# Windowed attention with two feed-forward stages on one Trainium2 core: diagonal matrices off GpSimd, weight remainders onto it, a third place for early scores, another idle fill

## Chip, core and metric

The kernel runs on one core of one Trainium2 chip. TensorE (PE in the profile), VectorE (DVE), ScalarE (ACT), GpSimd (POOL) and SyncE (SP, which issues most transfers) each work through a queue of their own in order. The metric is device time in microseconds (us) from a run of the whole program; lower is better.

## What is computed

Three layers follow one another, all in float32 from inputs that arrive partly as 64-bit floats:

```python
# attention: batch 4, 8 heads, 576 positions, 64 per head, window 64
scores = q @ k.T / sqrt(64)            # masked: 0 <= row - col < 64
attn = softmax(scores)                 # denominator + 1e-9
x = (attn @ v), heads side by side     # (4, 576, 512)
# first feed-forward stage
x_prev = x shifted by one position
xk = mu_k * x + (1 - mu_k) * x_prev
xr = mu_r * x + (1 - mu_r) * x_prev
k = relu(xk @ w_k)                     # 512 -> 1024
x = sigmoid(xr @ w_r) * (k * k @ w_v)  # 1024 -> 512
# second stage
gate = sigmoid(causal 5-tap convolution of x, per channel)
out = (gate * (x @ w_val)) @ w_out
```

## The kernel before

All 2,304 positions are cut into five blocks: t = 0 with 256 positions, then four of 512. In each block the attention has four units (one for two heads), so unit u = 0 to 3 belongs to block 0, u = 4 to 7 to block 1, and so on. A unit is a chain of small steps: `qk` (TensorE: scores with the mask added), `top` (VectorE: row maximum), `exp` (ScalarE), `eps` (one addition to the sums), `rec` (VectorE: reciprocal). In block 0 `diag` then makes diagonal matrices of the reciprocals, `tp` (TensorE) multiplies the scores by them, which transposes and normalizes at once, `pt` copies the result out of PSUM, `pv` (TensorE) multiplies by v and `x` copies the result to `xT`. In later blocks `norm` and a VectorE transpose `tr` take the place of `diag`, `tp` and `pt`.

The first stage of block t then needs, for each of xk and xr and each half g of the channels, `a` (the scaling by mu) and `xm` (VectorE: the mix with the shifted row). From block 1 on the mixed rows are split in a rounded part (`xhi`) and its remainder (`xlo`), and TensorE runs three float32r products; block 0 runs plain float32 products straight from the converted weights. The products are named r (w_r), h (w_k) and v (w_v); product m of block 0 comes in two halves.

Weights come as ten pieces: `ld` loads 64-bit words, `t` (VectorE shift), `g` (ScalarE) and `s` (VectorE) make float32 of them, `hi` rounds them and `lo` subtracts the rounded part from the whole, which gives the remainder. Only blocks 1 to 4 need `hi` and `lo`.

The order of everything is written out by hand: the table `SLOT` gives each step a place in one long list, and a letter says which engine takes it where there is a choice (a ScalarE, v VectorE, p GpSimd). The class `Plan` walks through that list, issues each step on its engine, and at the same time keeps its own estimate of the time; from that it decides where TensorE would wait for more than 400 ns, and calls `fill` there, which issues products of zeros into an unused PSUM tile. The estimates set nothing but the number of these. The scores of block 0 and of units 4 and 5 go into PSUM tiles of a pool `p0` with two buffers, but for unit 5, which has `s4`. When all of these are read, the pool is closed and its place becomes the four banks `pg` of the products.

Of the kernel before, what the change touches and what calls it, by code (L numbers as in the profile page):

```python
# [20 lines left out]
P = 128  # L21
# [22 lines left out]
    'first': '0',  # L44
    'warm': '1',
    'cap': '3',
    'ident': '2',
    'band': '13',
    'low': '4',
    'table': '12',  # L50
    'ldmu': '7',
    'ldc': '92',
    'mu': '51',
    'omu': '52',
    'pg': '79',
    'wc0': '323 250 326',
    'wc': '327',
    'first_x': '6',
    'ldqk': '8 9 10 14 16 49 101 127 161 150 195 256 328 338 367 414 406 433 461 528',
    'ldv': '15 30 60 68 87 110 139 181 289 235 305 322 386 390 432 453 507 505 550 607',  # L60
    'qk': '18 21 22 36 45 69 103 148 187 241 257 337 350 373 389 431 452 508 520 540',
    'top': '19 23 29 53 62 77 140 178 262 267 283 347 366 404 422 443 460 524 541 554',
    'exp': '20 25 33 55 71 78 147 191 269 281 297 355 375 408 428 454 468 531 552 557',
    'eps': 'v24 p26 v41 p59 p88 p112 p175 p192 v270 v282 v311 p365 v380 v410 p439 v464 p488 p543 p558 p565',
    'rec': '27 35 50 64 91 138 176 198 271 285 312 368 381 411 447 466 516 544 568 583',
    'diag': 'v28 p40 p57 p67',
    'tp': '34 44 61 73',
    'pt': 'v37 a46 v66 v82',
    'pv': '38 48 70 83 128 166 200 223 294 313 356 378 412 436 481 499 535 563 573 614',
    'x': 'v47 a56 v81 a84 a136 a182 a216 a238 v298 a317 a357 v384 v415 v444 a486 a502 a536 a567 a578 a643',  # L70
    'norm': 'v95 v154 v179 v215 v272 v306 a340 a371 a382 a426 v448 v495 v517 v545 v569 v595',
    'tr': '96 158 184 219 273 308 348 372 399 427 449 496 533 551 572 604',
    'mask': '107 160 194 246 274 344 354 374 405 434 459 513 534 553',
    'edge': '126 171 218 264 280 345 360 376 413 437',
    'a': 'a65 a85 a89 a113 a225 a228 a244 a248 a333 v334 a392 v393 a465 v471 a521 v523 a605 a610 a686 v711',
    'xm': '75 98 108 114 236 237 277 251 349 346 403 395 478 476 547 538 622 663 690 738',
    'xlo': '76 100 137 120 240 243 321 255 364 391 441 397 512 518 587 577 677 708 724 783',
    'carry': '118 123 278 295 363 420 522 570',
    'r': '80 105 86 121 93 119 102 116 336 339 342 352 462 483 501 494 655 695 681 692 801 824 826 827',
    'sig': '115 124 129 135 341 358 370 388 477 487 515 519 676 696 697 698 816 825 837 838',  # L80
    'h': '149 153 146 159 143 151 145 152 169 177 174 189 185 196 183 197 290 287 268 279 296 307 314 302 '
        '416 435 407 421 450 467 463 479 599 594 600 611 618 613 667 653 749 748 778 766 780 784 804 818',
    'relu': 'a155 a163 a157 a162 a204 a205 a206 a210 a291 a292 a286 a293 v318 v320 a331 a332 a442 a451 a429 '
        'v430 a474 a485 v484 a497 a602 v603 v617 a624 a649 v657 a668 v669 a756 v758 a779 a791 a793 v796 '
        'a817 a821',
    'sbuf': '164 165 208 211',
    'slo': 'a202 a203 a209 a212 310 325 330 353 472 480 503 510 629 642 684 679 792 808 829 828',
    'v': '220 230 213 233 226 253 254 259 359 383 361 377 401 417 400 402 525 555 537 561 566 580 514 532 '
        '712 735 699 710 706 720 747 752 866 884 831 851 843 853 860 882',
    'x2': '263 247 258 260 387 379 425 409 559 571 588 564 742 723 733 763 892 888 887 889',  # L90
    'st': '276 284 369 303 418 398 445 473 575 584 630 582 769 743 772 774 950 959 1000 987',
    'xhi': 'a239 a242 v319 v252 v362 v385 v440 a396 a511 a500 a576 a546 a672 v700 a716 v757',
    'cut': '232 249 343 394 475 530',
    'shi': '300 315 324 335 456 457 491 498 621 625 660 670 762 795 797 822',
    'sq': 'a301 a316 v329 a351 v469 a470 a492 v506 v628 a627 a683 a678 a777 v805 a819 v823',
    'staging': '5',
    'w_r ld': '11 42',
    'w_r g': '32 58',
    'w_r t': '31 63',
    'w_r s': '39 72',  # L100
    'w_r hi': 'a43 v90',
    'w_r lo': '54 94',
    'w_k ld': '104 74 125 131',
    'w_k g': '111 97 141 142',
    'w_k t': '117 106 156 170',
    'w_k s': '122 109 168 172',
    'w_k hi': 'v130 a134 a214 a222',
    'w_k lo': '180 144 227 229',
    'w_v ld': '133 132 173 193',
    'w_v g': '186 167 221 231',  # L110
    'w_v t': '188 190 199 217',
    'w_v s': '207 201 224 245',
    'w_v hi': 'a275 v288 a261 a265',
    'w_v lo': '309 304 299 266',
    'wide_x': '234',
    'turn': '836',
    'turn_s': '895',
    'turn_w': '865 845',
    'w_val ld': '542 562 597 647',
    'w_val room': '585 631 615 646',  # L120
    'w_val g': '586 633 619 654',
    'w_val t': '590 593 601 596 606 581 635 637 636 638 612 644 651 626 652 659 665 673 682 680',
    'w_val s': '592 634 620 661',
    'w_val hi': 'v608 a639 v662 a688',
    'w_val lo': '609 645 671 691',
    'w_val st': '616 632 648 658 666 675 717 705',
    'w_out ld': '640 694 740 746',
    'w_out room': '674 703 744 786',
    'w_out g': '687 704 745 787',
    'w_out t': '713 715 718 722 719 702 729 730 732 750 770 775 785 781 788 755 800 806 807 810',  # L130
    'w_out s': '714 721 771 798',
    'w_out hi': 'a726 v760 v789 a813',
    'w_out lo': '736 761 790 815',
    'w_out st': '759 751 767 773 809 802 814 835',
    'wv2': '867 839',
    'wo2': '902 880 881 848',
    'ldx': '841 904 926 1001',
    'gbuf': '871 922 1040 1034',
    'ldg': '873 949 1043',
    'xhi_': 'a846 v883 v855 a852 a879 a877 a910 a925 a909 a923 a948 a940 a972 a1056 a966 a982 a1002 a1009 a1075 '  # L140
        'a1106 a1077 a1090 v1124 v1105',
    'xlo_': '847 899 856 858 900 878 916 962 915 928 953 946 981 1061 991 983 1035 1021 1080 1118 1096 1102 '
        '1138 1110',
    'xsum': '842 849 859 876 906 911 924 934 958 964 994 1007 1070 1088 1103 1104',
    'val': '885 886 898 901 905 912 914 919 927 935 944 954 974 980 989 1066 999 1008 1028 1073 1044 1086 1098 '
        '1109 1114 1120 1135 1146',
    'valu': 'a891 a903 a907 a929 a945 a960 a996 a1016 a1031 a1100 a1112 a1127',
    'valc': '893 913 917 921 933 965 975 993 1068 1039 1082 1054 1108 1130 1140 1165',
    'gv': '894 920 918 932 973 978 986 1011 1069 1067 1089 1055 1164 1157 1142 1170',
    'ghi_': 'v896 a936 a930 a939 a943 a956 a967 a995 a1012 a1004 a992 a1006 a1022 a1025 a1093 a1062 a1101 v1113 '  # L150
        'a1116 v1144 a1132',
    'glo_': '897 937 979 942 947 971 968 1010 1026 1027 998 1015 1029 1033 1097 1072 1136 1122 1119 1145 1133',
    'gsum': '931 941 951 955 988 1003 1019 1024 1095 1115 1128 1131',
    'out': '908 952 963 969 976 985 997 1018 1030 1032 1048 1058 1081 1078 1099 1085 1123 1141 1143 1150 1156 '
        '1183 1185 1184 1188 1162 1168 1167 1173',
    'outu': 'a938 a970 a977 a1023 a1053 a1071 a1107 a1137 a1147',
    'o': '957 984 990 1005 1045 1074 1087 1079 1117 1148 1155 1163 1186 1189 1175 1169 1179',
    'os': '961 1017 1014 1037 1060 1076 1139 1092 1152 1158 1161 1171 1187 1190 1177 1174 1180',
    'oa': '1013 1051 1050 1064 1126 1125 1153 1178 1172',
    'tap': '1036 1041 1047 1038 1042 1052 1059 1065 1091 1046 1057 1084',  # L160
    'part': '1049 1020 1083 1111',
    'acc': '1063 1094 1121 1134',
    'gate': '1129 1154',
# [1167 lines left out]
```

## Time and profile before

| | |
|---|---|
| median of 3 runs (lowest, highest) | 413.92 us (413.46, 414.34) |
| the profiled execution: its time | 413.41 us |
| its span, first to last instruction | 411.5 us |
| TensorE busy | 402.6 us, 98% of the span |
| VectorE busy | 340.5 us, 83% |
| ScalarE busy | 261.5 us, 64% |
| GpSimd busy | 38.3 us, 9% |

Times in the rows below are microseconds from the start of the span unless marked ns. A matmul that the program issues in float32 stands twice in the trace, as two passes. [...]

### The profile page before, as it was taken

The page shows a single profiled execution, that of the slowest core. Times are in us where ns is not written, and L with a number is a line of the kernel's source. Part 1 is how long each engine was busy: PE and PEld are TensorE (multiplying, and loading weights), DVE is VectorE, ACT ScalarE, POOL GpSimd, SP SyncE. Part 2 cuts the span into 40 slices and gives each one's busy share as a digit, 9 for nine tenths or more (in the row PEclk, how much of TensorE's full clock was granted, in tenths as well). Part 3 has the DMA queues.
Part 4 walks back from the last instruction along what each step waited for, and adds up shares of the span by engine and source line. Part 5 has one row for each costly group of instructions (what it writes and reads, how often), then busy time and mean ns, then how long its engine had stood idle before and what let it go on. Part 6 is the DMA issues. An engine that isn't in the chain of part 4 may idle for free.

```text
span 411.5 us, 10921 instructions
## 1 busy us (share of the span) xinstructions
PE 402.6 (98%) x4587; PEld 342.1 (83%) x4587; DVE 340.5 (83%) x503; ACT 261.5 (64%) x607; POOL 38.3 (9%) x87
## 2 busy tenths in 40 slices
PE   8899999999999999999999999999999999999995
PEld 4678888887778778877888888888888999999995
DVE  4899999798548489789898899788885999999960
ACT  4889995778884767686556653156322476977531
POOL 3920101000100011000000000000000001123110
PEclk9999999999999999999999999999999999999999
DMA  7998911214323342262266428564999727869664
GB/s 284 411 414 339 328 46 57 78 44 145 107 74 129 98 125 77 78 223 92 80 242 263 149 89 291 208 235 156 405 395 382 261 86 245 228 142 198 137 149 128
DMA packets 24674, 78.37 MB, mean 190 GB/s; under 512 B 3376, under 2 KB 6704, under 8 KB 21808
## 3 DMA queue, kind: packets, MB, share of 16 engines
q1 hardware_dynamic: 22608, 72.64, 48.8%
q0 software_dynamic: 1872, 5.01, 7.3%
q8 instruction: 36, 0.59, 0.6%
q14 instruction: 14, 0.11, 0.1%
q10 hardware_dynamic: 144, 0.00, 0.0%
HBM read 51.80 MB, written 23.49 MB: 183 GB/s over the span
## 4 chain that ended last, share of the span: by engine, by line
PE 95%; POOL 3%; DVE 1%; ACT 0%; issue 0%; ACTq 0%; POOLq 0%
PE v L683 22%; PE h L683 21%; PE r L683 11%; PE sv L596 5%; PE h L706 4%; PE v L706 4%; PE sv L551 3%; PE val1m L961 3%; PE val3m L961 3%; PE out L1073 3%; PE out2m L961 3%; PE out1m L961 3%; PE val2m L961 3%; PE out0m L961 3%; PE val0m L961 3%; POOL rk L451 2%
## 5 line engine op out<-in xcount | busy, mean ns | idle before, releaser
L683 PE MATMUL h<-x,wk 128*128 128x512 f32 x384 | 90.5, 392 | 0.0
L683 PEld LDWEIGHTS h<-x,wk 128*128 128x128 f32 x384 | 71.6, 188 | 15.0
L683 PE MATMUL v<-sh,wv 128*128 128x512 f32 x256 | 82.4, 394 | 0.0
L683 PEld LDWEIGHTS v<-sh,wv 128*128 128x128 f32 x256 | 48.0, 188 | 10.8
L427 ACT ACTIVATE s<-s,m 128x96 f32<-128x96 f32 x120 | 43.0, 362 | 12.6 <-DVE m L416 11.5
L683 PE MATMUL v<-sl,wv 128*128 128x512 f32 x128 | 49.9, 390 | 0.0
L683 PE MATMUL r<-x,wr 128*128 128x512 f32 x192 | 45.8, 393 | 0.0
L683 PEld LDWEIGHTS r<-x,wr 128*128 128x128 f32 x192 | 35.7, 188 | 7.8
L892 DVE SCALAR_TENSOR_TENSOR early<-early,wc 128x576 f32<-128x576 f32 x48 | 38.5, 813 | 3.2 <-ACT early L890 2.7
L733 ACT ACTIVATE rk<-h 128x512 f32<-128x512 f32 (+1 forms) x30 | 15.4, 534 | 25.4 <-PE h L683 21.9
L683 PEld LDWEIGHTS v<-sl,wv 128*128 128x128 f32 x128 | 24.0, 188 | 4.7
L596 PEld LDWEIGHTS sv<-pt,vt 32*64 32x64 f32 x1536 | 18.9, 130 | 6.0 <-issue 3.9
L427 ACT ACTIVATION_READ_ACCUMULATOR s<-s,m 128x1 f32 x120 | 22.8, 190 | 0.0
L643 DVE SCALAR_TENSOR_TENSOR xm<-xT,omu,xm 128x512 f32<-128x512 f32 x32 | 22.3, 745 | 0.4 <-POOL xT L649 0.3
L666 DVE TENSOR_TENSOR x<-xm,x 128x1024 fp32r<-128x1024 f32 x16 | 19.5, 1219 | 3.6 <-ACT x L663 3.5
L785 DVE TENSOR_TENSOR sgs<-v,sgs 128x512 f32<-128x512 f32 (+1 forms) x20 | 12.5, 633 | 11.5 <-PE v L683 10.9
L763 DVE TENSOR_TENSOR sl<-rk,sh 128x1024 fp32r<-128x1024 f32 x16 | 19.5, 1221 | 2.4 <-ACT rk L761 2.2
L596 PE MATMUL sv<-pt,vt 32*64 32x32 f32 (+2 forms) x1536 | 20.8, 238 | 0.3 <-issue 0.3
L584 DVE STREAM_TRANSPOSE pt<-s 128x768 f32<-128x768 f32 x16 | 15.6, 973 | 5.1 <-ACT s L439 4.8
L757 ACT ACTIVATE sh<-rk 128x1024 fp32r<-128x1024 f32 x16 | 16.8, 1055 | 1.0 <-DVE rk L735 0.9
L896 ACT ACTIVATE early<-early 128x1152 f32<-128x1152 f32 x6 | 7.0, 1169 | 15.8 <-DVE early L892 15.8
L773 ACT ACTIVATE sgs<-r 128x512 f32<-128x512 f32 (+1 forms) x20 | 10.5, 552 | 8.2 <-PE r L683 8.1
(212 smaller groups left out, 828.0 us busy)
## 6 DMA issues: line engine op xcount, KB each, us to landing
qk<-qk SPq DMA_DIRECT2D x16, 544.0 KB, 5.1
vt<-vh SPq DMA_DIRECT2D x16, 384.0 KB, 3.9
xb<-x2d SPq DMA_DIRECT2D x4, 1152.0 KB, 6.7
out_t<-st SPq DMA_DIRECT2D x15, 288.0 KB, 2.9
w_out<-w SPq DMA_DIRECT2D x8, 512.0 KB, 3.4
w_val<-w SPq DMA_DIRECT2D x8, 448.0 KB, 3.1
wk<-w_val SPq DMA_DIRECT2D x2, 1792.0 KB, 8.8
early<-x2d SPq DMA_DIRECT2D x6, 576.0 KB, 4.4
```

What stands on the lines that cost most here:

```text
L427: ACT.activation(out=s, in_=scores()[:, 2 * c // n_s, c % (n_s // 2), :] if scores else s, func=AF.Exp, scale=D ** -0.5 if scores else 1.0 ...
L584: V.transpose(out=a["pt"][:, :m2 * KW], in_=a["s"].rearrange("p c j -> p (c j)"))
L596: PE.matmul(a["o"][heads[h], i, j0 * HW:j1 * HW], lhsT=a["v"][r, k, heads[h]], rhs=p, start=k == 0, stop=k == m + 1, skip_group_check=True)
L643: V.scalar_tensor_tensor(out=m, in0=xT[:, f, :n], scalar=omu[:, c:c + 1], in1=m, op0=ALU.mult, op1=ALU.add)
L666: lambda E: E.tensor_tensor(out=dst(1), in0=src(), in1=f32(dst(0)), op=ALU.subtract))
L683: PE.matmul(ps, lhsT=a, rhs=b[:, kt, :], start=(kt == 0 and i == 0), stop=(kt == nk - 1 and i == 2))
L706: PE.matmul(Ps[key][:, :n], lhsT=ws(kt), rhs=x()[:, kt, :], start=kt == 0, stop=kt == nk - 1)
L733: ACT.activation(out=o, in_=ps, func=AF.Relu)
L757: ACT.activation(out=Ss[t][0][:, f, :n], in_=rk(), func=AF.Square)
L763: lambda E: E.tensor_tensor(out=Ss[t][1][:, f, :n], in0=rk(), in1=f32(Ss[t][0][:, f, :n]), op=ALU.subtract))
L892: V.scalar_tensor_tensor(out=o, in0=x, scalar=c, in1=o, op0=ALU.mult, op1=ALU.add)
L961: PE.matmul(z[bank][:, j, :HS], lhsT=lhs, rhs=rhs, start=new and kt == 0 and e == 0, stop=kt == 1 and e == 2, skip_group_check=not new)
```

## The change

Six things change, and the diff shows them in this order.

- The table of places and letters is new throughout. `diag` of units 1 to 3 goes from GpSimd to VectorE, so all four are there. The remainder `lo` goes to GpSimd for both pieces of w_r, two of w_k and two of w_v; before, all ten were on VectorE.
- `masks` also copies a block of zeros into a part of `wr[1]` that is written for good only later.
- In `weight`, `lo` may run on VectorE or GpSimd. In `softmax`, `diag` may run on ScalarE or VectorE; no letter in the table picks ScalarE.
- The scores of units 2 and 5 use `s4`, those of 0, 1, 3 and 4 the two buffers of `p0` (function `space`). Products may take the place of `p0` once units 0 and 3 are read, and those with m > 1 of block 0 wait for units 1 and 4 instead.
- `tp` no longer waits for the `pv` before it; `pt` does.
- `fill` runs only in the stage before the later units, writes to the tiles of `tp` and `pv`, and past 6 us, when neither tile is held and no product is in PSUM, it multiplies halves of 64 rows by 256 columns of float32r zeros in place of 128 rows by 512 columns of bf16.

```diff
-    'diag': 'v28 p40 p57 p67',
-    'pt': 'v37 a46 v66 v82',
+    'diag': 'v27 v42 v49 v62',
+    'pt': 'v38 v50 a63 a79',
...
-    'w_r lo': '54 94',
+    'w_r lo': 'p69 p116',
...
-    'w_k lo': '180 144 227 229',
+    'w_k lo': 'v224 p203 p232 v226',
...
-    'w_v lo': '309 304 299 266',
+    'w_v lo': 'v347 v270 p294 p264',
...
+        G.tensor_copy(wr[1][:, NF - 1, :TA], warm)
     op("cap", "pool", 1300, ["warm"], masks)
...
-        vg((key, "lo"), n, [(key, "hi")],
-           lambda E: E.tensor_tensor(out=dst[1], in0=s(), in1=f32(dst[0]), op=ALU.subtract))
+        rest = lambda E: E.tensor_tensor(out=dst[1], in0=s(), in1=f32(dst[0]), op=ALU.subtract)
+        plan.any((key, "lo"), [(key, "hi")], ("dve", v_ns(n), lambda: rest(V)), ("pool", 8000, lambda: rest(G)))
...
-                 ("pool", 1300, lambda: [G.tensor_scalar(out=o, in0=ident, scalar1=l(1)[:, c:c + 1], scalar2=None, op0=ALU.mult)
-                                         for o in [diag()] for c, o in enumerate([o[:, c] for c in range(n_s)])]),
+                 ("act", 290 * n_s, by_act),
...
+    def space(u):
+        return Q["s4"] if u % 3 == 2 else p0.tile([P, 2, TB], F32, tag="p0", name=f"qk{u}")
...
-            a["ps"] = p0.tile([P, 2, TB], F32, tag="p0", name=f"qk{u}")
+            a["ps"] = space(u)
...
-        op(("tp", u), "pe", 870, [("diag", u), *([("pv", u - 1)] if u else [])], tp, ring=("pa", ("pt", u)))
+        op(("tp", u), "pe", 870, [("diag", u)], tp, ring=("pa", ("pt", u)))
...
-        plan.any(("pt", u), [("tp", u)],
+        plan.any(("pt", u), [("tp", u), *([("pv", u - 1)] if u else [])],
...
-    op("pg", "none", 0, [("exp", u) for u in range(HP + 1)], products)
+    op("pg", "none", 0, [("exp", 0), ("exp", 3), After(("exp", 1)), After(("exp", 4))], products)
...
-        if "pg" in Q:
-            if "spare" not in Q:
-                Q["spare"] = Q["pg"].tile([P, TB], F32, tag="g", name="spare")
-            ps = Q["spare"]
-        elif "ps" not in A[HP + 1]:
-            ps = Q["s4"][:, 0]
-        elif len(held) < 2:
-            ps = Q["pv" if "tp" in held else "tp"]
-        else:
+        if "sv" in Q or len(held) > 1:
             return
-        zero = warm.bitcast(BF16)
-        for _ in range(n):
-            PE.matmul(ps[:, :TB], lhsT=zero[:, :P], rhs=zero, start=True, stop=True)
+        ps = Q["pv" if "tp" in held else "tp"]
+        if len(Ps) or held or t < plan.COLD:
+            zero = warm.bitcast(BF16)
+            for _ in range(n):
+                PE.matmul(ps[:, :TB], lhsT=zero[:, :P], rhs=zero, start=True, stop=True)
+            return
+        zero = wr[1][:, NF - 1, :TA]
+        for i in range(n):
+            r = slice(i % 2 * W, i % 2 * W + W)
+            PE.matmul(Q["pv" if i % 2 else "tp"][:, :TA], lhsT=zero[r, :P], rhs=zero[r], start=True, stop=True)
```

Line numbers move by 8 to 15 in the changed file: VectorE's `diag` is L453 before and L464 after, its remainder L375 and L382.

How the order on three engines moves. On GpSimd, from the end of the masks, before (`first_m` and `m` hold the sums of a unit, `rk` the diagonal matrices, `s` the scores of a later unit):

```order
L324 COPY band<-cap 32x96 x4
L432 TENSOR_SCALAR first_m<-first_m 128x4
L451 TENSOR_SCALAR rk<-ident,first_m 128x128 x8
L432 TENSOR_SCALAR first_m<-first_m 128x4
L451 TENSOR_SCALAR rk<-ident,first_m 128x128 x4
```

and now:

```order
L325 CAST wr_66<-sgs 128x256
L440 TENSOR_SCALAR first_m<-first_m 128x4 x3
L332 COPY band<-cap 32x96 x4
L440 TENSOR_SCALAR m_324<-m_324 128x8
L382 TENSOR_TENSOR wr_66<-words,wr_65 128x4x256
L585 MEMSET s_540 32x2x64
L585 MEMSET s_540 32x2x32
L382 TENSOR_TENSOR wr_66<-words,wr_65 128x4x256
L585 MEMSET s_668 32x2x64
L585 MEMSET s_668 32x2x32
L382 TENSOR_TENSOR wk_64<-words,wk_63 128x4x256
```

The twelve diagonal pieces are gone, and remainders of 1,024 columns stand ahead of the small `edge` memsets of units 6 and 7 (`s_540`, `s_668`).

On VectorE, from the copy `pt` of unit 0, before (`x0` and `words` hold the first piece of w_r):

```order
L506 COPY pt0_242<-tp_157 128x512
L356 SCALAR_TENSOR_TENSOR words_141<-words_141,x0_139 128x1024
L432 TENSOR_SCALAR first_m_99<-first_m_99 128x4
L462 COPY xT_100<-pv_158 128x256
L435 RECIPROCAL first_m_99<-first_m_99 128x4
L340 TENSOR_SCALAR omu_60<-sm_59 128x8
L418 TENSOR_REDUCE first_m_99<-qk3_248 128x4
```

and now (`m4_324` are the sums of unit 4):

```order
L520 COPY pt0_304<-tp_145 128x512
L464 TENSOR_TENSOR rk_71<-ident_58,first_m_99 128x512
L443 RECIPROCAL first_m_99<-first_m_99 128x4
L426 TENSOR_REDUCE m4_324<-qk4_259 128x8
L427 TENSOR_SCALAR m4_324<-m4_324 128x8
L464 TENSOR_TENSOR rk_71<-ident_58,first_m_99 128x512
L520 COPY pt1_332<-tp_145 128x512
L362 TENSOR_SCALAR x0_117<-x0_117 128x1024
L443 RECIPROCAL first_m_99<-first_m_99 128x4
L364 SCALAR_TENSOR_TENSOR words_119<-words_119,x0_117 128x1024
L476 COPY xT_100<-pv_146 128x256
L381 CAST wr0_65<-words_119 128x4x256
```

The diagonal matrices of units 1 and 2 now stand between the copies, and the conversion of the weights behind them.

On SyncE, the first loads before (`early` and `qk4` take q and k of a unit, `sgs` and `rk` take v, `x0` and `s0` pieces of w_r):

```order
L400 DMA early_73<-qk 128x576 x3
L369 DMA x0_139<-w_r 128x2048
L400 DMA early_73<-qk 128x576
L406 DMA sgs_72<-vh 128x512
L400 DMA qk4_154<-qk 128x1088
```

and now:

```order
L408 DMA early_73<-qk 128x576 x4
L408 DMA qk4_174<-qk 128x1088
L414 DMA sgs_72<-vh 128x512
L377 DMA x0_117<-w_r 128x2048
L414 DMA rk_71<-vh 128x512
```

The first piece of w_r is loaded behind the queries of units 3 and 4 and the values of unit 0.

## Rows read from the trace of the kernel before

**Rows 1.** The page: TensorE's busy time; data moved in 40 slices of the span.

```profile
PE 402.6 (98%) x4587; PEld 342.1 (83%) x4587; DVE 340.5 (83%) x503; ACT 261.5 (64%) x607; POOL 38.3 (9%) x87
...
GB/s 284 411 414 339 328 46 57 78 44 145 107 74 129 98 125 77 78 223 92 80 242 263 149 89 291 208 235 156 405 395 382 261 86 245 228 142 198 137 149 128
```

**Rows 2.** Waits: all of TensorE's from 24 us on.

```profile
PE sv L596 <- issue: 0.3, 1, 0.3
```

**Rows 3.** Waits: all of VectorE's from 22 to 70 us.

```profile
DVE sgs L785 <- PE v L706: 0.5, 1, 0.5
```

**Rows 4.** The chain that ended last: start, us, engine, what.

```profile
10.61 2.67 POOL rk L451 x3
...
13.82 3.93 POOL rk L451 x4
...
18.41 3.63 POOL rk L451 x4
...
22.57 0.86 PE r L706 x4
```

**Rows 5.** Timeline of TensorE: start, us, operation, count.

```profile
32.55 2.86 PE L706 MATMUL h<-x,words 128*128 128x256 f32 x12
...
69.37 11.27 PE L683 MATMUL h<-x,wk 128*128 128x512 f32 x48
```

**Rows 6.** Timeline of VectorE from 8 to 21 us.

```profile
8.22 0.69 DVE L453 TENSOR_TENSOR rk<-ident,first_m 128x512 f32<-128x512 f32 x1
8.83 0.68 DVE L418 TENSOR_REDUCE first_m<-qk 128x4 f32<-128x512 f32 x1
...
9.73 0.70 DVE L354 TENSOR_SCALAR x<-x 128x1024 int32<-128x1024 int32 x1
10.34 0.17 DVE L435 RECIPROCAL first_m<-first_m 128x4 f32<-128x4 f32 x1
10.42 0.66 DVE L506 COPY pt<-tp 128x512 f32<-128x512 f32 x1
11.00 1.22 DVE L356 SCALAR_TENSOR_TENSOR words<-words,x 128x1024 int32<-128x1024 int32 x1
...
12.42 0.42 DVE L462 COPY xT<-pv 128x256 f32<-128x256 f32 x1
...
13.76 1.22 DVE L375 TENSOR_TENSOR wr<-words,wr 128x1024 fp32r<-128x1024 f32 x1
15.52 0.96 DVE L418 TENSOR_REDUCE m<-qk 128x8 f32<-128x768 f32 x1 [0.54 <-PE qk L551]
16.51 0.17 DVE L419 TENSOR_SCALAR m<-m 128x8 f32<-128x8 f32 x1
...
18.93 1.22 DVE L356 SCALAR_TENSOR_TENSOR words<-words,s 128x1024 int32<-128x1024 int32 x1
20.07 0.99 DVE L643 SCALAR_TENSOR_TENSOR x<-xT,omu,x 128x256 f32<-128x256 f32 x2
```

**Rows 7.** ScalarE's groups from 0 to 26 us: count | busy us, mean ns.

```profile
L427 ACT ACTIVATE xm<-qk,first_m 128x128 f32<-128x128 f32 x16 | 5.6, 373 | 3.6 <-DVE first_m L419 3.6
...
L427 ACT ACTIVATE s<-qk,m 128x96 f32<-128x96 f32 x8 | 2.7, 431 | 0.0
...
L630 ACT ACTIVATE x<-xT,sm 128x256 f32<-128x256 f32 x5 | 2.3, 558 | 0.0
...
L351 ACT ACTIVATE words<-x 128x1024 f32<-128x1024 f32 x1 | 1.2, 1200 | 0.6 <-DMA x<-w_r 0.6
```

**Rows 8.** Loads issued from 2.10 to 2.42 us: KB, us to landing.

```profile
x<-w_r SPq DMA_DIRECT2D x1, 1024.0 KB, 7.6
```

**Rows 9.** Diagonal pieces on GpSimd running at 18.9 to 19.1 us: ns, first and last start.

```profile
L451 POOL TENSOR_SCALAR rk<-ident,first_m x2: 602/1120/1637, 18.4 to 19.0; 128x128 f32<-128x128 f32 x2
```

**Rows 10.** The mix at 20 us on VectorE: the first one, then both.

```profile
L643 DVE SCALAR_TENSOR_TENSOR x<-xT,omu,x x1: 597/597/597, 20.1 to 20.1; 128x256 f32<-128x256 f32 x1
...
L643 DVE SCALAR_TENSOR_TENSOR x<-xT,omu,x x2: 475/536/597, 20.1 to 20.6; 128x256 f32<-128x256 f32 x2
```

More of the change, by code (lines that the diff above doesn't have):

```diff
@@ L43, with __init__ @@
 SLOT = {
[71 rows of a table removed]
[71 rows of a table added]
     'wide_x': '234',
     'turn': '836',
[57 rows of a table removed]
-}
[57 rows of a table added]
+}
+class After:
+    def __init__(self, key):
+        self.key = key
 class Plan:
@@ L218, in run @@
         for (key, _, deps, ring, tab, moves), w in self.ordered():
-            ready = [*deps]
+            ready = [d for d in deps if not isinstance(d, After)]
+            assert all(d.key in end for d in deps if isinstance(d, After))
             if ring and len(used[ring[0]]) >= self.rings[ring[0]]:
@@ L235, in run @@
                 new = max(link, end[key] + self.START) + moves
-                link = new + self.STALL * (link < self.RAMP <= new)
+                link = new + sum(n for at, n in self.STALLS if link < at <= new)
                 end[key] = link + self.LAND
@@ L487, in qk @@
                               rhs=a["k"][heads[h], c * W:c * W + P], start=False, stop=True, skip_group_check=True)
-        op(("qk", u), "pe", 728, [("ldqk", u), "low", "idle"], qk, ring=("p0", ("exp", u)))
+        op(("qk", u), "pe", 728, [("ldqk", u), "low", "idle"], qk, ring=("p0" if u % 3 < 2 else "s4", ("exp", u)))
         def s_of():
@@ L535, in qk @@
         def qk():
-            a["ps"] = Q["sv"] if not early_scores else Q["s4"] if u > HP else p0.tile([P, 2, TB], F32, tag="p0", name=f"qk{u}")
+            a["ps"] = Q["sv"] if not early_scores else space(u)
             if early_scores:
@@ L554, in unit @@
         if early_scores:
-            op(("qk", u), "pe", 1360, [("ldqk", u), "low", "idle"], qk, ring=("s4" if u > HP else "p0", ("exp", u)))
+            op(("qk", u), "pe", 1360, [("ldqk", u), "low", "idle"], qk, ring=("p0" if u % 3 < 2 else "s4", ("exp", u)))
         else:
@@ L767, in r_tile @@
         product(("r", t, m), wr, lambda: X[t]["r"],
-                lambda c: [("xlo", t, g, "r") for g in ((0, 1) if t else (c,))] + [(("w_r", m // 2), "lo" if t else "s")],
+                lambda c: [("xlo", t, g, "r") for g in ((0, 1) if t else (c,))] + [(("w_r", m // 2), "lo" if t else "s")]
+                + ([("exp", 1), ("exp", 4), *[After(("r", 0, i, 0)) for i in range(2)]] if t == 0 and m > 1 and c == 0 else []),
                 ("sig", t, m))
```

12 lines of the change are left out of this document (8 added, 4 removed), and 246 rows, old and new, of the table SLOT.

## The prediction

> **What bounds the kernel now.** I read the page first: TensorE is busy for 402.6 of 411.5 us [rows 1]. Its waits from 24 us on add up to 0.3 us [rows 2]. So nothing after 24 us can get shorter unless work is taken away, and this change takes no product away but those of zeros at the start. What can move is how early the unbroken stretch begins. The chain that ended last says what it begins after: three times it goes through diagonal matrices made on GpSimd, 2.67, 3.93 and 3.63 us, and only then the first r product starts at 22.57 us [rows 4]. From there TensorE runs through r, from 32.55 us through h and v of block 0, and at 69.37 us starts the products of block 1 [rows 5].
>
> The second thing to see is VectorE. From 22 to 70 us it waits for 0.5 us in all [rows 3]. It is as full as TensorE there, so whatever lengthens its queue shows up as a late TensorE.
>
> **The change part by part.** *Diagonal matrices.* On VectorE one takes 0.69 us, and the next operation starts 0.61 us after it [rows 6]; on GpSimd the twelve pieces took 10.2 us together [rows 4]. This removes the chain. Next in line for the first r product is VectorE's own queue, up to the first mix `xm`. I add it up in its new order from the start of the diagonal matrix of unit 0 at 8.22 us, which nothing in the change moves. Steps go from start to start of rows 6:
>
> - diagonal of unit 0 0.61; maximum of unit 2 with its scaling 0.90; reciprocal 0.08; the same pair for unit 3 0.90; copy of unit 0 0.58: 3.07
> - diagonal 1 0.61; reciprocal 0.08; maximum of unit 4 0.99, scaling 0.08; diagonal 2 0.61; copy of unit 1 0.58: 2.95
> - conversion of the first piece of w_r: shift 0.61, reciprocal 0.08, merge 1.14; `x` of unit 1 0.34 (0.42 less the usual 0.08 of overlap); rounding taken as the shift of the same size, 0.61: 2.78
> - diagonal 3 0.61; maximum of unit 5 0.99, scaling 0.08; the mix of two halves 0.91: 2.59
>
> That is 11.39 us, so the mix is done at 19.61 and r starts at about 19.65 instead of 22.57: **2.9 us earlier**.
>
> This holds if nobody else is late. ScalarE: `exp` of units 2 and 3 take 1.4 us each (16 pieces, 5.6 us [rows 7]) from 9.75, so to 12.6; a copy 0.35, the conversion 1.2 to 14.2 [rows 7], wanted at 14.9; unit 4's `exp` 2.7 to 16.9; a copy taken as VectorE's 0.66 [rows 6]; two scalings 0.93 (five take 2.3 [rows 7]) to 18.5, wanted at 18.7. That margin is 0.2 us. Loads: w_r's first piece landed 7.6 us after 2.11, at 9.7 [rows 8]. It now stands behind 1,088 KB more (units 3 and 4's q and k, unit 0's v). The second slice moves 411 GB/s [rows 1], so it comes 2.7 us later, at 12.4, wanted by ScalarE at 13.0. The load costs nothing as long as that holds; without this cover each us late is a us on r.
>
> From r to h TensorE has the same eight halves, one `pv`, one `qk` and another `pv` in both, 32.55 - 22.57 = 9.98 us, so it asks for h at 29.6. VectorE has to mix three more times by then. In the new order that is: `x` twice 0.68, shift twice 1.22, merge twice 2.28, three operations on 768 columns at 0.9 (the maximum of that width took 0.96), three mixes at 0.8 (the pair at 20.07 less its delay, below), four small ones 0.32: 9.6 us, ready at 29.2. TensorE is just behind, by **0.4 us**. So the lead of 2.9 us is kept, and hardly more could be.
>
> *Remainders.* Six of 1.22 us (the subtraction at 13.76 [rows 6]) leave VectorE. Between r and block 1's first product three of them lie (3 x 1.14 = 3.4 us); a normalization and a PSUM copy go to ScalarE (about 1.5), while two scalings and two relus come from it (about 2.2). VectorE's queue is 2.7 us shorter there. That alone saves nothing, since TensorE is full; it is slack. On GpSimd a remainder has no row. The nearest is a diagonal piece of 128 columns, 0.6 us undisturbed and 1.64 beside a long operation of VectorE [rows 9], so eight of them are 4.9 to 13.1 us; nearest to a busy VectorE is the mean of the chain's, 0.95 each [rows 4], and I take 7.6 us. Block 1 needs them far later. But the memsets `edge` of units 6 and 7 are queued behind the two of w_r, then the maximum of the unit on VectorE, and all that stands behind it.
>
> *What the two engines cost each other.* Of two pieces on GpSimd from 18.41 on, the first took 0.60 us and the second, from 19.0, 1.64 [rows 9]: it began just behind VectorE's merge (18.93 to 20.15 [rows 6]) and ended 0.5 us after it. GpSimd waited. The first mix on VectorE behind it took 597 ns, the second 475 [rows 10]: VectorE waited too, 0.12 us, the only such case that I found. A remainder reads 2 x 1,024 columns where that piece read 128. So it costs VectorE between 0.12 us (a short collision) and 16 x 0.12 = 1.9 us (every column read counts). A collision shortens nothing, so there is no gain below. I take a value in the lower part, about 0.3 us: of the two delays GpSimd's, 1.04 us, is the nine times longer. Of five remainders up to block 1, two fall before h, where the margin is 0.4; the other three meet the slack. Loss: about 0.4 us.
>
> The Trainium skill, SBUF — State Buffer, section "SBUF: two separate sides", says the port pair that the two share is an exclusive lock for a whole instruction. Rows 10 agree only if GpSimd's hold is its reading time, not its 0.6 us.
>
> *The rest.* A third score place lets units 2 and 3 be computed earlier; VectorE's queue is what they wait for, so 0. Zeros copied on GpSimd stand behind the masks: 0. `pt` in place of `tp` waiting for `pv`: 0, VectorE is behind. The fill is work in TensorE's gaps: 0, unless the clock falls.
>
> **Sum.** 413.41 (the profiled execution) - 2.9 + 0.4 = 410.9 us. That execution lies 0.5 us under the median of the runs shown, so I expect a median of 411.4 us.
>
> **Rivals.**
>
> 1. *GpSimd's reading holds VectorE, slower.* At the full 1.9 us each: the first remainder starts behind diagonal 3, has the maximum of unit 5 beside it (PSUM, one operand) and holds the mix by 0.9 us; the second holds h by 1.9 less the margin of 0.4; the lead at h is 2.9 - 0.9 - 1.5 = 0.5. Three more cost 5.7, the slack takes 2.7, which leaves 3.0. Result: 2.5 us slower, a median of 416.4. It turns at about 1.3 us a remainder. For it: the 0.12 us of rows 10, scaled by the columns. Against: it is one event, and it scales a delay that may not grow with length.
> 2. *It eats the lead only.* With 1.0 to 1.5 us a remainder, as when a third of VectorE's operations read no second operand from SBUF: 413 to 414.5, no change.
> 3. *GpSimd late.* ScalarE from 18.5: a conversion 1.2, a copy 0.66, unit 5's `exp` 2.7, four scalings 1.9, a conversion 1.2, two scalings 0.9 and the rounding, taken as a conversion, 1.2; so w_r's second `hi` is there at 28.3. VectorE, from 29.2: two shifts, two merges, four operations on 768 columns, two relus and a rounding, 8.4 us, so it comes to the maximum of unit 7 at 37.6. A second remainder of up to 9.3 us is done by then. At 13.1 us each, the first runs from 17.0 to 30.1 and the second to 43.2, and VectorE stands for 5.6 us, which is the lead and the slack together: 413.9, no change, and with any of rival 1 slower, up to 419. It decides from 9.3 us a remainder; eight times 0.95 is 7.6.
> 4. *Nothing moves.* ScalarE or the loads miss by 2 to 3 us, so r starts where it did: 413.5 to 414. Margins of 0.2 and 0.6 us speak for a part of it, the sums against the whole.
>
> **How the numbers follow.** Forecast 0.5, rival 1 0.17, rival 2 0.17, rival 3 0.08, rival 4 0.08. A change of 0.2% (0.83 us) is about what a measurement of this kernel can tell from none. The forecast's own range is 410.4 (all of 2.9, and a little more from what I took for margins) to 412.8. With the rivals: low 410.2, high 416.0; outside lie the upper halves of rivals 1 and 3. Faster: the forecast and a part of rival 2, 0.54; same: the rest of rival 2 and half of 3 and 4, 0.22; slower: rival 1 and the other halves, 0.24.
>
> **What would show it.** Right: first r product at 19.5 to 20.2 us, first h at 29.5 to 30.5, first float32r product at 66.5 to 67.5, no wait of TensorE over 0.5 us behind that. The chain at the start goes through VectorE, not GpSimd. Wrong by rival 1: operations on VectorE with two operands in SBUF last over 2 us while a remainder runs. By rival 3: VectorE waits for GpSimd's memset near 38 us. By the fill: a granted clock under 1.00 before 25 us. What would make me wrong outright is a gap in TensorE past 70 us, where the order is new too and no row speaks of it.

## The result: 1.4% slower

The changed kernel takes a median of 420.44 us (418.43 to 420.98, four runs), the kernel before 414.13 us beside it. The ratio is 1.0142, with a 95% interval of 1.0102 to 1.0182: 5.9 us slower (the two medians differ by 6.3), where the forecast was 2.5 us faster. Its profiled execution took 418.43 us, with a span of 416.6 us.

The page's line of busy times, against the first of [rows 1]:

```profile
PE 401.9 (96%) x4590; PEld 341.7 (82%) x4590; DVE 351.8 (84%) x515; ACT 249.7 (60%) x577; POOL 47.4 (11%) x83
```

TensorE has slightly less to do than before, and VectorE is busy 11.3 us longer although six remainders have left it and only three diagonal matrices of 0.69 us have come. The waits of TensorE from 24 us on, which answer to [rows 2] (for what: us in total, times, longest):

```profile
PE sv L610 <- issue: 1.7, 1, 1.7
PE v L720 <- DVE early L364: 1.3, 1, 1.3
PE sv L610 <- DVE s L576: 1.0, 1, 1.0
PE h L697 <- DVE sgs L800: 0.9, 2, 0.7
```

0.3 us of waiting has become about 5. The first row names no releaser, but it is VectorE's too: that product starts at 60.84 us, 0.1 us behind the end of the transpose that makes its operand (the row of 59.77 further down).

The chain of [rows 4] has the first r product at 22.57 us. In the timeline, by which I compare from here on, the kernel before starts it at 22.40:

```profile
22.40 1.03 PE L706 MATMUL r<-x,words 128*128 128x256 f32 x4
```

TensorE's timeline now, also against [rows 5], shows where the time goes:

```profile
20.09 0.38 PE L1286 MATMUL tp<-wr 64*128 64x256 f32 x1 [2.46 <-POOL wr L382]
...
22.01 1.03 PE L720 MATMUL r<-x,words 128*128 128x256 f32 x4
...
32.26 1.03 PE L720 MATMUL h<-x,words 128*128 128x256 f32 x4
...
53.68 5.42 PE L720 MATMUL v<-s,early 128*128 128x256 f32 x24 [1.27 <-DVE early L364]
...
74.03 2.32 PE L697 MATMUL h<-x,wk 128*128 128x512 f32 x9 [0.74 <-DVE sgs L800]
```

r and h start 0.4 and 0.3 us earlier than before, not 2.9, and the first float32r product comes 4.7 us later. Behind it almost nothing has changed: from there to the end of the span 342.1 us pass before and 342.6 now. The result lies ahead of 74 us, so in all that follows I read one number first, the start of the first float32r product.

GpSimd's remainders up to there are these (start, us):

```profile
17.37 2.66 POOL L382 TENSOR_TENSOR wr<-words,wr 128x1024 fp32r<-128x1024 f32 x1
29.98 2.60 POOL L382 TENSOR_TENSOR wr<-words,wr 128x1024 fp32r<-128x1024 f32 x1 [1.21 <-ACT wr L380]
41.59 2.35 POOL L382 TENSOR_TENSOR wk<-words,wk 128x1024 fp32r<-128x1024 f32 x1 [3.27 <-DVE wk L381]
53.06 5.58 POOL L382 TENSOR_TENSOR wk<-words,wk 128x1024 fp32r<-128x1024 f32 x1
69.75 2.39 POOL L382 TENSOR_TENSOR wv<-rk,wv 128x1024 fp32r<-128x1024 f32 x1
```

And this is VectorE at the same times:

```profile
17.74 0.95 DVE L426 TENSOR_REDUCE m<-s 128x8 f32<-128x768 f32 x1
18.72 1.34 DVE L427 TENSOR_SCALAR m<-m 128x8 f32<-128x8 f32 x1
19.98 0.87 DVE L657 SCALAR_TENSOR_TENSOR x<-xT,omu,x 128x256 f32<-128x256 f32 x2
...
30.39 2.86 DVE L657 SCALAR_TENSOR_TENSOR x<-xT,omu,x 128x256 f32<-128x256 f32 x2
...
42.23 2.26 DVE L362 TENSOR_SCALAR s<-s 128x1024 int32<-128x1024 int32 x1
...
54.06 1.22 DVE L364 SCALAR_TENSOR_TENSOR early<-early,words 128x1024 int32<-128x1024 int32 x1
55.19 1.22 DVE L364 SCALAR_TENSOR_TENSOR early<-early,x 128x1024 int32<-128x1024 int32 x1
56.33 3.52 DVE L657 SCALAR_TENSOR_TENSOR xm<-xT,omu,xm 128x512 f32<-128x512 f32 x2
59.77 0.96 DVE L598 STREAM_TRANSPOSE pt<-s 128x768 f32<-128x768 f32 x1
...
63.51 1.40 DVE L657 SCALAR_TENSOR_TENSOR xm<-xT,omu,xm 128x512 f32<-128x512 f32 x2
...
69.18 3.51 DVE L657 SCALAR_TENSOR_TENSOR xm<-xT,omu,xm 128x512 f32<-128x512 f32 x2
```

Look at where they end. The first remainder ends at 20.03 us; the scaling of eight columns, 0.17 us elsewhere, lasts 1.34 and ends at 20.06. The pair of mixes at 30.39 takes 2.86 us where the pair at 19.98, behind a remainder, takes 0.87, and the shift 2.26 instead of 0.69. What VectorE loses is 1.2, 2.0, 1.6 and, where a pair of 512 columns takes 3.5 instead of 1.4 us, twice 2.1: 9.0 us for five remainders ahead of the first float32r product. VectorE itself needs 1.14 each, 5.7 us. The maximum at 17.74, which reads PSUM, ran through untouched beside the first.

The hold goes both ways: the fourth remainder shows 5.58 us because VectorE's merges and shifts (the rows of 54.06 and 55.19) kept GpSimd waiting first, for an estimated 3.2 us if it then ran its usual 2.4.

### The profile page after: what moved, and what is told of

The parts are those of the page before. It is cut to its first block, busy times and chain, and to the rows that moved or that the text cites. A ratio compares the mean times of both kernels' runs of the same rounds, so it can differ in the third digit from the quotient of the medians.

```text
span 416.6 us, 10903 instructions
## 1 busy us (share of the span) xinstructions
PE 401.9 (96%) x4590; PEld 341.7 (82%) x4590; DVE 351.8 (84%) x515; ACT 249.7 (60%) x577; POOL 47.4 (11%) x83
## 4 chain that ended last, share of the span: by engine, by line
PE 78%; DVE 13%; ACT 3%; DMA 2%; issue 2%; POOL 1%; DVEq 0%; ACTq 0%; POOLq 0%
PE v L697 21%; PE h L697 19%; PE r L697 11%; PE sv L610 3%; PE val1m L976 3%; PE val3m L976 3%; PE out L1088 3%; PE out1m L976 3%; PE val2m L976 3%; PE out2m L976 3%; PE out0m L976 2%; DVE xm L657 2%; PE sv L565 2%; DMA xb<-x2d 2%; ACT s L435 1%
## 5 line engine op out<-in xcount | busy, mean ns | idle before, releaser
L657 DVE SCALAR_TENSOR_TENSOR xm<-xT,omu,xm 128x512 f32<-128x512 f32 x32 | 26.5, 872 | 0.0
L576 DVE SCALAR_TENSOR_TENSOR s<-sv,band 128x768 f32<-128x768 f32 x14 | 13.3, 949 | 8.2 <-PE sv L565 7.4
L788 ACT ACTIVATE sgs<-r 128x512 f32<-128x512 f32 (+1 forms) x20 | 10.6, 547 | 11.3 <-PE r L697 11.2
```

Source lines behind the costliest of these rows:

```text
L576: V.scalar_tensor_tensor(out=a["s"], in0=ps, scalar=D ** -0.5, in1=band[:, None, :].to_broadcast([P, m2, KW]), op0=ALU.mult, op1=ALU.min)
L657: V.scalar_tensor_tensor(out=m, in0=xT[:, f, :n], scalar=omu[:, c:c + 1], in1=m, op0=ALU.mult, op1=ALU.add)
```

## Experiments

Three theories: **A**, a remainder on GpSimd holds VectorE for as long as it runs, about 2 us; **B**, the fill's wait of 2.5 us for w_r's remainder, and what the clock does after it; **C**, the new order itself costs. Times are medians, ratios are to runs of the kernel before on the same chip.

### Without the six remainders: what the rest of the change is worth

The first run leaves the six subtractions out and lets the third product of each float32r triple read the rounded weights in place of the remainder, so that TensorE's work stays the same. In the second, w_r's two subtractions are back on GpSimd, and the fill is of bf16 zeros.

```diff
-("pool", 8000, lambda: rest(G))
+("pool", 8000, lambda: None)
...
+            wl = wh if wt is wr or wt is wk or wt is wv else wl
```

> The changed kernel without the six remainders that GpSimd takes; the third product of each float32r triple of the first stage reads the rounded weights again, so TensorE's work is the same (left out: the six subtractions and the use of the remainders of w_r, w_k and w_v). Nothing holds VectorE and the fill waits for nothing. This is the change as the prediction had it, with remainders that cost VectorE nothing. If the prediction's other steps stand: r at 19.7 to 20.8, h near 29.6, first float32r product at 66.5 to 67.5, time 410 to 411.5. If the new order by itself costs: first float32r product over 68.5, time 412.5 or more.

> The one before this with w_r's two remainders on GpSimd again and the fill of bf16 zeros alone (left out: the other four subtractions and the use of remainders in the first stage). Theory: VectorE is held by 1.2 us ahead of the first mix and by 2.0 us ahead of h, as in the changed kernel, so r is 1 to 1.3 us and h 2 to 3.2 us later than in the one before this; the first float32r product 2 to 3 us later. Rival: VectorE has slack behind h, so the first float32r product moves by less than 1 us.

The first took 411.51 us, ratio 0.9934 (0.9898 to 0.997); the second 412.56, 0.9976 (0.9953 to 0.9999). TensorE's timeline without the six:

```profile
19.48 1.05 PE L721 MATMUL r<-x,words 128*128 128x256 f32 x4
...
28.48 0.94 PE L610 MATMUL sv<-pt,vt 32*64 32x96 f32 x62 [1.08 <-issue]
...
31.18 1.03 PE L721 MATMUL h<-x,words 128*128 128x256 f32 x4
...
67.34 2.88 PE L698 MATMUL h<-x,wk 128*128 128x512 f32 x11
```

The forecast had 19.65, 29.6 and 66.5 to 67.5. So the change but for its remainders does what the sum said, h apart, and C by itself falls as an account of the loss; what the order costs with the six on VectorE is measured further down. With w_r's two back on GpSimd r starts at 20.69, h at 32.06 and the first float32r product at 68.98: 1.2, 0.9 and 1.6 us later. That is less than expected for h and the float32r product; h had been late by 1.1 us without any hold, and part of the second one may have fallen into that, which is not shown.

### Remainders back on VectorE, and the other fill

The first run has the upper edit (with `p203 p232` of w_k and `p294 p264` of w_v alike), the second the lower, the third both.

```diff
-    'w_r lo': 'p69 p116',
+    'w_r lo': 'v69 v116',
...
-        if len(Ps) or held or t < plan.COLD:
+        if True:
```

> The changed kernel with its six GpSimd remainders on VectorE again, at the same places of the list; the fill still reads the zeros in wr[1]. Theory A (a remainder on GpSimd holds VectorE for about 2 us, five of them before 72 us, and that is most of the 6.3 us lost): VectorE pays 1.14 us for each instead of about 2, and no operation of VectorE lasts over 1.5 us where its like takes 0.2 to 0.9; median 414 to 416. Theory B (the fill's wait of 2.5 us for the remainder of w_r is most of it): the fill now waits for VectorE's remainder, about 1 us, so 417.5 to 419. Theory C (the new order of the rest costs the time): 419 to 421.

> The changed kernel with the remainders on GpSimd, but the fill always of bf16 zeros from the tile that is never written again, so that it waits for no remainder. Theory A: VectorE is held as before, the first mix still ends near 20.9 us, so r starts near 21 and little is won after it; 418 to 420. Theory B: the idle time of 2.5 us at 17.6 us goes, and with it the granted clock under 1.00 of some runs; 415 to 416.5. Theory C: 419 to 421.

> The changed kernel with both edits: remainders on VectorE at their places, fill of bf16 zeros alone. Theories A and B together: what is left of the change is its order, its score places and VectorE's diagonal matrices; w_r's two remainders stand ahead of the first mix and of h on VectorE and take 1.1 us each of the 2.9 us won; 412.5 to 414.5. Theory C (the order itself costs): 416 or more.

Remainders back: 415.05 us, 1.0047 (1.002 to 1.0075). Other fill: 417.52, 1.0105 (1.008 to 1.013). Both: 414.72, 1.0038 (1.0025 to 1.0051), 0.2 us over the range expected. With the six on VectorE the scaling of eight columns takes 0.17 us again, and the first float32r product starts at 70.87 instead of 74.03: 3.2 us, against the 9.0 less 5.7 of the rows above. A is the larger part, though some of B goes with it in this run: the fill then waits for VectorE's shorter remainder. The fill alone is worth about 1.5 us by the ratios beside GpSimd's remainders, with intervals that overlap, and nothing measurable without them (1.0047 and 1.0038). In the profiled run of the second r starts at 20.61 us instead of 22.01, but the first float32r product only at 73.50 instead of 74.03: what the fill gives back, VectorE's holds mostly take. So B is a part at most; 417.52 lies between its range and A's.

### The remainders alone, in the order of before

```diff
-    'w_r lo': '54 94',
-    'w_k lo': '180 144 227 229',
-    'w_v lo': '309 304 299 266',
+    'w_r lo': 'p54 p94',
+    'w_k lo': 'v180 p144 p227 v229',
+    'w_v lo': 'v309 v304 p299 p266',
```

> The kernel before with six remainders on GpSimd (both of w_r, the second and third of w_k, the third and fourth of w_v) at their old places, and nothing else; diagonal matrices of units 1 to 3 stay on GpSimd. Theory A (a remainder on GpSimd holds VectorE for about 2 us where VectorE itself needs 1.14): slower than before by 2 to 5 us, with VectorE's operations on SBUF of 0.2 to 0.9 us lasting up to 3.3 us at five or six places; first float32r product 2 to 4 us later than 69.37. The diagonal pieces queue behind w_r's remainder on GpSimd too, so r can be 1 to 2.5 us later by itself. Rival (as the prediction had it: 0.3 us each, and VectorE's queue shorter by 5 us): 412.5 to 414.

421.76 us, 1.0165 (1.0127 to 1.0203): more than A allows. The timeline of TensorE says why:

```profile
16.79 6.85 PE L1272 MATMUL s<-sgs 128*128 128x512 bf16 x31
```

These are products of zeros. The planner's estimate of 8,000 ns for a remainder makes it foresee a long gap and fill it; the gap was short, and TensorE was kept busy until 23.6 us. The second run has an estimate of 2,500 ns.

> The kernel before with six remainders on GpSimd alone, as in the earlier run, but with an estimate of 2,500 ns for one in the planner instead of 8,000, so that the fill issues 23 products of zeros instead of 48 in the first stage. Theory: 31 of those stood in one row and kept TensorE busy from 16.8 to 23.6 us while the diagonal matrices were ready at about 19; without them r starts at 22.5 to 24.5 and what is left is the hold of VectorE: time 1.5 to 4 us over the kernel before (415 to 417.5). Rival: with the holds of about 2 us each the fill did not matter, r stays near 27: 420 or more.

417.69 us, 1.0097 (1.0065 to 1.0129): 4 us slower with nothing changed but the remainders' engine and that estimate, 0.2 us over the range expected. Two of the six, GpSimd's rows first and then VectorE's:

```profile
25.00 2.36 POOL L374 TENSOR_TENSOR wr<-words,wr 128x1024 fp32r<-128x1024 f32 x1 [1.67 <-DVE wr L373]
36.08 2.38 POOL L374 TENSOR_TENSOR wk<-words,wk 128x1024 fp32r<-128x1024 f32 x1 [4.17 <-DVE words L356]
...
25.07 3.11 DVE L442 TENSOR_TENSOR s<-s,m 128x768 f32<-128x768 f32 x1
36.11 2.90 DVE L373 CAST wk<-words 128x1024 fp32r<-128x1024 f32 x1
```

Started 0.03 to 0.07 us behind a remainder, operations of 0.95 and 0.69 us last 3.11 and 2.90: each is held for 2.2 us, until the remainder ends. So the hold is shown here without the new order and without the fill's wait. Not all of the 4 us is the hold, though: a part is GpSimd's own queue, in which the diagonal matrices of units 2 and 3 now stand behind w_r's first remainder.

```profile
19.43 3.62 POOL L451 TENSOR_SCALAR rk<-ident,first_m 128x128 f32<-128x128 f32 x4 [0.38 <-PE tp L499]
...
23.43 1.03 PE L706 MATMUL r<-x,words 128*128 128x256 f32 x4
```

Those of unit 3 start 1.0 us later than in [rows 4], and r with them. That is 1.0 of the 4.3 us by which the first float32r product is late (73.66); the other 3.3 come behind r.

### Four short remainders, and two late ones

The first run cuts each of GpSimd's remainders into four of 256 columns; the second has bf16 fill and gives GpSimd only the two of w_v that run behind the first float32r product (`'w_v lo': 'p347 v270 p294 v264'`).

> The changed kernel, but each remainder on GpSimd is four instructions of 256 columns instead of one of 1,024. If the hold lasts as long as one GpSimd instruction: no operation of VectorE is late by more than about 0.7 us, but three or four in a row are, so the sum per remainder stays near 2 us and the time stays at 418 to 421. If a held operation of VectorE pays once per remainder whatever its length, the loss falls to a quarter: first float32r product 2 us earlier than 74.0, time 416 to 418.

> The changed kernel with bf16 fill and all remainders on VectorE but two of w_v, which GpSimd takes behind the first float32r product, where VectorE is no longer full (8.3 of 10 us busy from 70 to 80). Theory: each holds VectorE for up to 2.3 us again, with operations of 0.4 to 0.9 us lasting up to 3 us, but VectorE has the room: first float32r product as without them (70.0 to 70.9), time within 0.8 us of 414.7. Rival: the hold costs wherever it falls: 1 to 3 us longer, and TensorE waits for VectorE behind 75 us.

In quarters: 418.56 us, 1.0109 (1.0079 to 1.014). VectorE beside the first four (the pair and the scaling take 0.87 and 0.17 us alone):

```profile
18.31 0.40 DVE L430 TENSOR_SCALAR m<-m 128x8 f32<-128x8 f32 x1
18.63 1.89 DVE L660 SCALAR_TENSOR_TENSOR x<-xT,omu,x 128x256 f32<-128x256 f32 x2
```

0.2 and 1.0 us lost make the same 1.2 as in one piece, only spread; the first float32r product is at 73.79. The hold lasts as long as a GpSimd instruction (a quarter takes 0.71 us at the least), and short ones follow on one another. Whether quarters help a little stays open: the intervals of this run and of the changed kernel overlap, and in this profiled run the granted clock fell to 0.50 from 22 to 24 us.

The two late ones: 414.52 us, 1.003 (1.0008 to 1.0052), against 1.0038 without them; first float32r product 70.42. Where VectorE has room a hold costs nothing that these runs can tell. In the first of them VectorE keeps GpSimd waiting, which then holds a scaling (0.72 us) and neither the transpose nor the relu from PSUM ahead of it:

```profile
83.20 0.96 DVE L450 TENSOR_TENSOR s<-s,m 128x768 f32<-128x768 f32 x1
84.26 0.98 DVE L598 STREAM_TRANSPOSE pt<-s 128x768 f32<-128x768 f32 x1
85.16 0.65 DVE L749 TENSOR_SCALAR rk<-h 128x512 f32<-128x512 f32 x1
85.74 0.72 DVE L440 TENSOR_SCALAR m<-m 128x8 f32<-128x8 f32 x1
...
83.19 3.24 POOL L382 TENSOR_TENSOR wv<-early,wv 128x1024 fp32r<-128x1024 f32 x1 [2.33 <-issue]
```

### The clock behind the fill's wait

The changed kernel again, unedited:

> The changed kernel as it is, beside the same runs of the kernel before as the three others. Theory: 5 to 7 us over before (ratio 1.012 to 1.018); the runs that show a granted clock of 0.99 are 1 to 3 us longer than those with 1.00, because TensorE's 2.5 us without work ahead of the fill is followed by a stretch at half clock in some runs. Rival: the clock has no part in it; times do not go with it.

418.79 us, 1.0139 (1.009 to 1.0188). Its four runs are 421.13, 419.82, 417.69 and 417.75 us at mean granted clocks of 0.988, 0.994, 0.999 and 0.999. The profiled one is the first. Its windows (busy us and count of each engine, granted clock, DMA share, GB/s):

```profile
18.00:20.00 2.00, 0.00 (x0) 0.00 (x0) 1.97 (x3) 1.13 (x1) 2.00 (x1) 0.98 1.05 425
20.00:21.00 1.00, 0.90 (x9) 0.68 (x11) 0.85 (x3) 0.00 (x0) 0.04 (x1) 0.50 0.95 382
...
25.00:26.00 1.00, 1.00 (x14) 0.63 (x14) 0.00 (x0) 1.00 (x8) 0.00 (x0) 0.50 1.11 446
26.00:27.00 1.00, 1.00 (x12) 0.86 (x9) 0.46 (x2) 1.00 (x8) 0.00 (x0) 0.63 0.92 380
...
56.00:58.00 2.00, 1.19 (x4) 1.02 (x5) 2.00 (x3) 2.00 (x9) 1.92 (x3) 0.86 0.59 232
58.00:60.00 2.00, 2.00 (x6) 1.62 (x5) 2.00 (x3) 2.00 (x5) 2.00 (x1) 0.50 0.03 7
```

TensorE does nothing from 18 to 20 us, as in the run shown first, but here the granted clock falls to 0.50, the 1.2 GHz level, until about 26.7 us, and again near 58 us behind TensorE's wait for a held VectorE. This second fall does not need the fill's wait: the profiled run with bf16 fill shows 0.50 from 54 to 56 us as well. r starts at 23.52 us instead of 22.01, the first float32r product at 77.16 instead of 74.03. So one and the same wait of 2.5 us costs 3 us more in some runs, and that fits the first four: the three with clocks of 0.996, 0.996 and 0.988 lie about 2 us over the one with 0.999.

### Diagonal matrices alone, and w_r's remainders later

The first run is the kernel before with `'diag': 'v28 v40 v57 v67'`. The second also moves w_r's remainders behind the first mix and behind all four of r. The third drops the four products of zeros ahead of r as well.

```diff
         if "pg" in Q:
-            if "spare" not in Q:
-                Q["spare"] = Q["pg"].tile([P, TB], F32, tag="g", name="spare")
-            ps = Q["spare"]
+            return
```

> The kernel before with the diagonal matrices of units 1 to 3 on VectorE, at their old places, and nothing else. The term of the prediction that a chain through GpSimd sets r: r starts 1.5 to 3 us earlier, 411 to 412.5. Rival (VectorE's queue takes it all back, since three matrices of 0.61 us stand ahead of other steps there, and its remainder of w_r too): r within 0.7 us of 22.57, 413.3 to 414.5.

> The kernel before with the diagonal matrices on VectorE, and w_r's two remainders, still on VectorE, moved back: the first behind the first mix, the second behind the four mixes of r. Theory (VectorE's queue sets r once GpSimd's chain is gone, each remainder ahead of a mix costs 1.14 us): the first mix ends near 19.5 us, unit 4's exp on ScalarE near 20.7 and four products of the fill then set r, at 21.6; h, whose mixes no longer have a remainder ahead, at 30.7 to 31.2 instead of 31.9; total 0.5 to 1.2 us under the one with the diagonal matrices alone. Rival (VectorE is full up to 70 us, so what is moved only comes back before the first float32r product): no difference from it, within 0.3 us, and TensorE waits for VectorE somewhere from 32 to 68 us.

> The one before this, without the four products of zeros that stand ahead of the first r product. Theory: they start at 20.7 when unit 4's exp lets the banks go and keep r waiting for 0.86 us, so r starts near 20.8 and the time is another 0.5 to 0.9 us shorter if VectorE keeps up. Rival: r starts earlier but h waits for its mixes on VectorE, so nothing is won; or the idle time ahead of r lowers the granted clock and 1 to 2 us are lost.

413.82 us, 1.002 (0.9998 to 1.0042); 413.98, 0.9982 (0.996 to 1.0004); 414.4, 1.0006 (0.9981 to 1.0031). None is told apart from before, which for the first is the rival by its time. r starts at 21.60, 22.26 and 20.72 us (22.40 before), the first float32r product at 68.33, 71.17 and 70.63 (69.37 before). The first profiled run, the fastest of its ten at 411.93 us, kept its lead; the median does not show one. In the second a load of queries was 0.6 us late for TensorE, and 1.1 and 1.5 us of waiting, for which the profile names no releaser, stand near 37 us in the second and third: in the third an r 1.7 us earlier is given back before h of block 1.

### What stays of the loss: VectorE's queue

With remainders on VectorE and bf16 fill 1.6 us stay (1.0038). The first run moves five letters to ScalarE (two scalings, where the expectation counted one), the second also w_r's remainders behind the mixes of r and behind the first h; the third moves only the remainders.

```diff
-    'a': 'a66 a90 a97 a108 v171 v196 a239 a244',
-    'relu': 'v145 v150 a172 a180',
-    'w_k hi': 'a221 v153 v195 a222',
+    'a': 'a66 a90 a97 a108 a171 a196 a239 a244',
+    'relu': 'a145 a150 a172 a180',
+    'w_k hi': 'a221 v153 a195 a222',
```

> The changed kernel with remainders on VectorE, fill of bf16 zeros, and four more steps ahead of block 1 on ScalarE instead of VectorE: one scaling of block 1, two relus of block 0, one rounding of w_k (about 2 us of VectorE's queue less what they overlap). Theory: what is left of the loss without GpSimd's remainders (1.6 us) is VectorE's longer queue, which TensorE waits for by 2.2 us between 24 and 70 us; most of these waits go, first float32r product at 68.5 to 69.7 instead of 70.46, time 1 to 2 us shorter, about that of the kernel before. Rival: ScalarE, as full there, becomes what TensorE waits for: first float32r product 70 to 72, time as without this edit or longer.

> The one before this, with w_r's two remainders behind the four mixes of r and behind the first h, still on VectorE. Theory that VectorE is full up to the first float32r product: r and h come up to 1 us earlier, the first float32r product does not move by more than 0.5 us, no difference in time. Rival: the lead is kept; time another 1 us shorter.

> The changed kernel with all remainders on VectorE, fill of bf16 zeros, and w_r's two remainders behind the four mixes of r and behind the first h. If what a remainder of 1.14 us ahead of the mixes costs is carried on to the first float32r product, r and h come 1 to 1.5 us earlier and the first float32r product at 69.0 to 69.8 instead of 70.46: time 412.8 to 414, level with the kernel before. If VectorE's queue up to the first float32r product decides, that product stays at 70.2 to 70.8 and the time at 414 to 415.

417.6 us, 1.0105 (1.0071 to 1.0138): the rival. TensorE's waits of that run:

```profile
PE sv L610 <- ACT wk L380: 1.3, 1, 1.3
PE v L720 <- DVE rk L364: 1.2, 1, 1.2
PE h L720 <- ACT rk L747: 0.9, 2, 0.7
```

Two of the three moved kinds, the rounding of w_k and the relu, are now what TensorE waits for; ScalarE has no room there. The second: 416.65 us, 1.0088 (1.0061 to 1.0116), first float32r product at 71.78 instead of 73.08, so the lead of 1.4 us was kept, against my theory. The third: 414.66, 1.0037 (1.0012 to 1.0063). There r and h start 1.3 us earlier than with the remainders at their places (20.25 and 30.51), yet the first float32r product is at 70.56 against 70.46: all of it is given back, as TensorE waits for VectorE by 3.0 us behind r. There VectorE's queue as a whole decides, not the place of w_r's remainders. Why the second run kept its lead is open. No version that makes all ten remainders is told apart as faster than the kernel before.

## Why the prediction was wrong

- **The chain through GpSimd, and VectorE's queue in its new order: the times were right, the path in part.** Without remainders r started at 19.48 us, or 19.65 in the chain's count that the forecast's 19.65 goes by. The first mix started at 18.81 us, by the sum at 18.70. But the chain of that run leaves VectorE at 14.3 us, with the copy of unit 1, and reaches r through TensorE's own products, which end just as the mixes do (19.68): that the two meet is partly luck. Two readings were off without harm: the 10.2 us of [rows 4] are eleven of the twelve pieces, and 9.98 us from r to h mixes two views; the timeline alone has 10.15.
- **h at 29.6: 1.6 us too early.** Without remainders it was 31.18. TensorE waited 1.1 us in the middle of a `pv` that I had counted as work alone; the profile names no releaser. The lead at h was 1.4 us and not the 2.9 that I said would be kept, and 2.0 at the first float32r product, so the right time of that run is partly luck too.
- **"A value in the lower part, about 0.3 us" for a collision: the step that failed.** Five remainders cost VectorE 9.0 us, 1.8 each, near the upper bound of 1.9 us. I chose between the bounds by one event of 0.12 us, because GpSimd's delay there was the longer one. That says nothing of how VectorE's delay grows with what GpSimd reads; my own scaling by columns read, 16 times 0.12, came close. Rival 1, at 0.17, was the mechanism, its sign included: operations of VectorE over 2 us beside a remainder. Its 416.4 us fell 4.0 us short; the fill and the clock are a part of that, the rest was not taken apart.
- **The Trainium skill, SBUF — State Buffer, section "SBUF: two separate sides"**, has the shared port pair locked for whole instructions. I weakened that to GpSimd's reading time. For remainders the rows agree with the plain rule: a cast started 0.03 us behind a remainder ended 0.55 us behind its end, 2.90 us for 0.69. [rows 9] and [rows 10] do not by themselves: GpSimd's piece ended 0.57 us behind the start of a mix that lost 0.12. No run here takes that case apart.
- **"The fill is work in TensorE's gaps: 0, unless the clock falls": wrong as well.** The zeros stand in `wr[1]`, which w_r's first remainder writes earlier in the order; so the fill waits for that remainder, 2.46 us, ahead of the `pv` and `tp` that r needs, and the chain at the start still goes through GpSimd. I had the two lines in the diff and did not put them together. The sign that I named, a granted clock under 1.00 before 25 us, showed in one profiled run of two. Worth about 1.5 us by the medians of the run with bf16 fill, whose interval overlaps, and 0.5 us in the traces at the first float32r product.
- **VectorE's queue 2.7 us shorter: right only while GpSimd's work is free.** Without remainders the kernel gained 0.66%, 2.7 us of 414.09, about the 2.5 us of the forecast. With the six on VectorE the new order loses 1.6.
- **GpSimd late (rival 3): no.** A remainder that did not wait takes 2.4 to 2.7 us, not 7.6. Eight pieces of 128 columns at 0.6 us and more are no measure for 1,024 columns of another operation: a quarter of a remainder, 256 columns, takes 0.71 us at the least.
- **No gap behind 70 us: right.** From the first float32r product to the end 341.1 to 342.7 us pass in all kernels here.

## What to carry to other kernels

Before work goes from a full engine to an idle one, ask what the two share: here GpSimd took 1.14 us of work off VectorE and stopped it for up to 2.2. Where VectorE had room that cost nothing; no run here shows that it pays. And a filler must read and write nothing that real work touches, and is no better than the planner's estimate of the gap: twice a product of zeros was what held TensorE up.

## What the runs showed of the hardware

- A two-input GpSimd operation of 1,024 columns takes 2.35 to 2.66 us where it does not wait, and shifts, casts, mixes and scalings of VectorE from SBUF to SBUF, even one of eight columns, wait until it ends: 1.2 to 2.2 us lost each time. A maximum that reads PSUM (0.95 us) and a transpose within SBUF (0.98 us) ran beside it at full speed.
- GpSimd can wait through several operations of VectorE in a row: one remainder lasted 5.58 us beside merges and shifts that followed one another.
- The same stretch of TensorE without work does not always lower the granted clock: 18 to 20 us empty gave 1.00 throughout in one run and 0.50 for 6.7 us in another of the same kernel.
